# A third of the feed-forward units moved onto the score ring while attention runs

## Chip, core and metric

One core of a Trainium2 chip runs the whole program. The metric is device time in microseconds (us) of one execution; lower is better. TensorE is called PE below, VectorE DVE, ScalarE ACT, GpSimdE POOL, and the queue that issues the transfers SP, as in the profile.

## What is computed

```python
def reference(q, k, v, g_q, g_k, moe_w_in, moe_w_out, moe_s, moe_b, moe2_w_in, moe2_w_out):
    # q, k, v: 4 batches, 12 heads, 448 positions, 64 wide, float32
    q_n, k_n = rmsnorm(q, g_q), rmsnorm(k, g_k)
    attn = softmax(q_n @ k_n.T / sqrt(64))
    x = (attn @ v) gathered to 1792 tokens x 768
    h = x @ moe_w_in                       # 768 -> 2048
    x = (s * relu(h)**2 + b) @ moe_w_out   # 2048 -> 768
    h = x @ moe2_w_in
    return (h * cos(h)) @ moe2_w_out
```

Both feed-forward layers are computed with each operand split in a high and a low part, so each product is three matmuls (high by high, high by low, low by high).

## The kernel before

Attention goes by pairs of heads: 24 pairs, four score steps each, 96 steps in all. A step multiplies 112 rows of queries with all 448 keys for the two heads (tiles `sc`, line 193, two banks of PSUM), takes the row maximum on DVE (`top`, L205) and the exponential on ACT (`pr`, L208). Two steps later PE turns those rows over (`tp`, L226), and ACT copies the one head and DVE the other to SBUF (`pT`, L232 and L230). Once in a pair come the transposes of the next pair's queries and keys (`pt_q`, `pt_k`, L173), that of the reciprocals (`rt`, L237) and the product with the values (`av`, L249).

A feed-forward unit of the first layer is either an in-unit (`ph`, L400: 18 matmuls into one bank, from one block of 128 hidden columns and one batch) or an out-unit (`po`, L452: 6 matmuls into one bank, from a chunk of two such blocks). After an in-unit ACT takes the relu (`r`, L411), POOL squares it (L413), DVE scales it (`gt`, L415), ACT rounds it to its high part (`gh`, L429) and POOL makes the low part (`gl`, L430); `gh` and `gl` are what the out-units of that chunk read. After an out-unit ACT copies (first chunk, L458) or DVE adds (L461) the bank into `acc`. Weights are loaded ahead by `load_weight` into three buffers of each part (`wh`, `wl`): ACT writes the high part (L338), POOL the low part (L339), in two halves of 384 columns.

The first nine pairs run alone. From then on the generator of attention steps and the list of feed-forward units are woven by rates, until the attention is done; the last units of that stretch are those of segment 2. After that the score and transpose banks are given back and six banks with the tags `ph` and `po` (pool `psb`) take their place for the rest.

While attention runs PSUM's eight banks are: two with the tag `mo` (pool `psm`), four with the tag `sc` and two with the tag `tp`. In the woven part all feed-forward units share the two `mo` banks, the scores the four `sc` banks, and `pt`, `tp`, `rt` and `av` the two `tp` banks. The order on each engine is not that of the code: a scheduler sets it when the program is built, and each engine then runs its list in order, waiting on semaphores. A tile takes its bank when the scheduler places its first instruction, so a unit that has no bank is placed later than units behind it.

Of the kernel before, what the change touches and what calls it, by code (L numbers as in the profile page):

```python
# [33 lines left out]
def body(ctx, tc, q, k, v, g_q, g_k, w1_in, w1_out, s_in, b_in, w2_in, w2_out, out):  # L34
# [27 lines left out]
    psm = ctx.enter_context(tc.tile_pool(name="psm", bufs=2, space=PSUM))  # L62
# [28 lines left out]
    pools = {}  # L91
# [9 lines left out]
    def products(w, x):  # L101
        return ((w[0], x[0]), (w[1], x[0]), (w[0], x[1]))
# [229 lines left out]

    weights = {}
    plain = {}
    count = {"g": 0, "raw": 0}

    def halves(w, wh, wl, eng=nc.gpsimd):
        nc.scalar.copy(wh, w)  # L338
# [46 lines left out]
    g = {}  # L385
    acc = {}
    visits = {}
    pair = []

    def unit_in(layer, seg, ck, f, b):  # L390
        ft = ck * CF + f
        key = f"{layer}_{ft}_{b}"
        wh, wl = weights[layer, seg, 0, ft, 0]
        wh, wl = (z.rearrange("p (c f) -> p c f", f=P) for z in (wh, wl))
        pool, tag, bufs = (pools["psb"], "ph", 3) if "psb" in pools else (psm, "mo", 2)
        ph = pool.tile([P, 512], F32, tag=tag, name=f"ph_{key}", bufs=bufs)
        h = ph[:, :S]
        for c in range(NE):
            for n, (a, m) in enumerate(products((wh[:, c, :], wl[:, c, :]), xs[layer, b][c])):
                nc.tensor.matmul(h, a, m, start=(c == 0 and n == 0), stop=(c == NE - 1 and n == 2))  # L400
            if c % 2 and c < NE - 1:
                yield 1.13
        if count["g"] % 2 == 0:
            n = count["g"] // 2
            gp, nb = (ma, 3) if "mb" not in pools or n % 5 < 3 else (pools["mb"], 2)
            pair[:] = [gp.tile([P, 2, S], F32R, tag=f"g{z}", name=f"g{z}_{key}", bufs=nb) for z in "hl"]
        gh, gl = (z[:, count["g"] % 2, :] for z in pair)
        count["g"] += 1
        if layer == 0:
            r = ma.tile([P, S], F32, tag="t0", name=f"r_{key}")  # L410
            nc.scalar.activation(r, h, AF.Relu)  # L411
            r2 = ma.tile([P, S], F32, tag="t1", name=f"r2_{key}")
            nc.gpsimd.tensor_tensor(r2, r, r, ALU.mult)  # L413
            gt = ma.tile([P, S], F32, tag="t2", name=f"gt_{key}")
            nc.vector.tensor_scalar(gt, r2, sb[:, 0:1], sb[:, 1:2], ALU.mult, ALU.add)  # L415
        else:
            hs = ma.tile([P, S], F32, tag="t0", name=f"hs_{key}")
            nc.scalar.copy(hs, h)  # L418
            h = hs
            kk = ma.tile([P, S], F32, tag="t1", name=f"kk_{key}")  # L420
            nc.scalar.activation(kk, h, AF.Copy, scale=1.0 / (2 * math.pi), bias=MAGIC)
            nc.scalar.activation(kk, kk, AF.Copy, bias=-MAGIC)
            gt = ma.tile([P, S], F32, tag="t2", name=f"gt_{key}")
            nc.vector.scalar_tensor_tensor(gt, kk, -C1, h, ALU.mult, ALU.add)
            nc.vector.scalar_tensor_tensor(gt, kk, -C2, gt, ALU.mult, ALU.add)  # L425
            nc.scalar.activation(gt, gt, AF.Abs)
            nc.scalar.activation(gt, gt, AF.Sin, scale=-1.0, bias=halfpi)  # L427
            nc.gpsimd.tensor_tensor(gt, h, gt, ALU.mult)  # L428
        nc.scalar.copy(gh, gt)  # L429
        nc.gpsimd.tensor_tensor(gl, gt, gh.bitcast(F32), ALU.subtract)  # L430
        g[ft, b] = (gh, gl)
        if layer == 1 and b % 2:
            g[ft, "pair", b // 2] = [z.rearrange("p b s -> p (b s)") for z in pair]
        yield 1.13
# [3 lines left out]
        yield 1.13  # L438

    def po_tile(key):  # L440
        pool, tag, bufs = (pools["psb"], "po", 3) if "psb" in pools else (psm, "mo", 2)
        return pool.tile([P, 512], F32, tag=tag, name=f"po_{key}", bufs=bufs)

    def unit_out_1(seg, ck, et, b):
        key = f"0_{ck}_{et}_{b}"
        cols = et % (NE // 2)
        w = weights[0, seg, 1, ck, et // (NE // 2)]
        w = [z.rearrange("p (f c e) -> p f c e", f=CF, e=P)[:, :, cols, :] for z in w]
        po = po_tile(key)[:, :S]
        for f in range(CF):  # L450
            for n, (a, m) in enumerate(products([z[:, f, :] for z in w], g[ck * CF + f, b])):
                marks["out"] = nc.tensor.matmul(po, a, m, start=(f == 0 and n == 0), stop=(f == CF - 1 and n == 2))  # L452
        visits[et, b] = visits.get((et, b), 0) + 1
        if visits[et, b] == 1:
            if et % 2 == 0:
                acc[et // 2, b] = ma.tile([P, 2 * S], F32, tag="acc", name=f"acc_{key}", bufs=NE)
            at = acc[et // 2, b][:, et % 2 * S:(et % 2 + 1) * S]
            nc.scalar.copy(at, po)  # L458
            return
        at = acc[et // 2, b][:, et % 2 * S:(et % 2 + 1) * S]  # L460
        nc.vector.tensor_tensor(at, po, at, ALU.add)  # L461
        if visits[et, b] < NCK:
            return
        if b < 2:
            t = dram.tile([P, S], F32, tag=f"y_{b}_{et}", name=f"yd_{b}_{et}")
            nc.sync.dma_start(t, at)
            stash[1, b, et] = t
        else:
            xs.setdefault((1, b), []).append(split(at, xa, f"2_{b}_{et}", nc.vector if et % 4 < 2 else nc.gpsimd))

    def unit_out_2(seg, ck, eh, t):
        key = f"1_{ck}_{eh}_{t}"
        w = [z.rearrange("p (f e) -> p f e", f=CF) for z in weights[1, seg, 1, ck, eh]]
        pr, j0 = t // NT, t % NT * P
        po = po_tile(key)[:, :EH]
        for f in range(CF):
            x = [z[:, j0:j0 + P] for z in g[ck * CF + f, "pair", pr]]
            for n, (a, m) in enumerate(products(x, [z[:, f, :] for z in w])):
                nc.tensor.matmul(po, a, m, start=(f == 0 and n == 0), stop=(f == CF - 1 and n == 2))  # L479
        if ck == 0 and eh == 0:  # L480
            pool, nb = (ma, NE) if t < NE else (pools["mb"], 2 * NT - NE)
            acc[t] = pool.tile([P, E], F32, tag="acc", name=f"acc_{key}", bufs=nb)
        at = acc[t][:, eh * EH:(eh + 1) * EH]
        if ck == 0:
            nc.scalar.copy(at, po)
        else:
            nc.vector.tensor_tensor(at, po, at, ALU.add)  # L487
        if ck < NCK - 1 or eh == 0:
            return
        j = j0  # L490
        while j < j0 + P:
            b, c, p = 2 * pr + j // S, j % S // CP, j % CP
            n = min(CP - p, j0 + P - j)
            rows = out[b * S:(b + 1) * S, :].rearrange("(p c) e -> c p e", c=NCH)[c, p:p + n, :]
            nc.sync.dma_start(rows, acc[t][j - j0:j - j0 + n, :])
            j += n
# [153 lines left out]
```

## Time and profile before

| | us |
|---|---|
| median of three runs | 1315.49 |
| lowest and highest of them | 1313.4, 1315.62 |
| the profiled execution, device time | 1311.19 |
| its span, first to last instruction | 1309.4 |
| PE busy in that span | 1246.8 |

The profile tells of one execution. "Busy" of an engine is the time in which at least one of its instructions ran; the matmuls of a stream overlap, so the distance of their starts, not their length, is what one of them costs. The mean granted clock of PE over the span is 0.996 of full speed.

### The profile page before, as it was taken

How to read it: one execution, taken by the hardware profiler on the slowest of the kernel's cores; microseconds unless marked ns; L12 is line 12 of the kernel's file. 1: busy time of each engine (PE TensorE's matmuls, PEld its weight loads, DVE VectorE, ACT ScalarE, POOL GpSimd, SP SyncE). 2: the span in 40 equal slices, each digit the busy share in tenths (PEclk: the TensorE clock that was granted, in tenths of full speed). 3: DMA queues.
4: the chain of work that ended last, by engine and by line, in shares of the span. 5: the costliest groups of instructions: out<-in, count | busy, mean ns of one | idle time of the engine just before them, and what ended most of it. 6: DMA issues, size and time to landing. Idle time of an engine off the chain costs nothing.

```text
span 1309.4 us, 18684 instructions
## 1 busy us (share of the span) xinstructions
PE 1246.8 (95%) x6624; PEld 1033.3 (79%) x6624; DVE 845.8 (65%) x1452; ACT 755.4 (58%) x1694; POOL 569.6 (43%) x624
## 2 busy tenths in 40 slices
PE   5998899899999999999999999999999999999998
PEld 2444565676776767779999999989999999999997
DVE  5787674867768685754454445764767767666655
ACT  5787685666556655534432224788656657565641
POOL 3445454644536524234332223555544435354531
PEclk9999999999999999999999999999999999999999
DMA  3324252433433333253221222121212211111105
GB/s 102 94 87 125 83 151 59 137 123 115 125 113 104 120 104 114 68 185 117 89 70 49 66 63 64 47 61 49 66 32 73 66 56 49 49 50 49 49 13 169
DMA packets 81534, 111.33 MB, mean 85 GB/s; under 512 B 7200, under 2 KB 71456, under 8 KB 81440
## 3 DMA queue, kind: packets, MB, share of 16 engines
q1 hardware_dynamic: 81440, 110.13, 28.0%
q8 instruction: 52, 0.85, 0.3%
q14 instruction: 42, 0.34, 0.1%
HBM read 86.51 MB, written 23.59 MB: 84 GB/s over the span
## 4 chain that ended last, share of the span: by engine, by line
PE 67%; ACT 11%; DVE 10%; DMA 5%; POOL 3%; issue 3%; SPq 0%; ACTq 0%; DVEq 0%; POOLq 0%
PE ph L400 26%; PE po L479 14%; PE po L452 13%; PE av L249 5%; PE sc L193 4%; PE tp L226 3%; ACT pr L208 3%; DMA raw<-in_moe_w_out_dram 2%; DVE t L375 2%; DVE top L205 2%; DMA xr<-xd 1%; DMA raw<-in_moe_w_in_dram 1%; DVE gt L425 1%; ACT c L371 1%; ACT pT L232 1%
## 5 line engine op out<-in xcount | busy, mean ns | idle before, releaser
L400 PE MATMUL ph<-xh,wl 128*128 128x448 f32 x768 | 282.8, 368 | 0.0
L400 PE MATMUL ph<-xh,wh 128*128 128x448 f32 x768 | 280.1, 369 | 2.3 <-ACT hs L418 2.2
L400 PE MATMUL ph<-xl,wh 128*128 128x448 f32 x768 | 281.9, 368 | 0.0
L430 POOL TENSOR_TENSOR gl<-gt,gh 128x448 fp32r<-128x448 f32 x128 | 158.9, 1246 | 184.4 <-ACT gh L429 184.3
L339 POOL TENSOR_TENSOR wl<-t,wh 128x384 fp32r<-128x384 f32 x128 | 138.5, 1102 | 78.7 <-ACT wh L338 78.6
L208 ACT ACTIVATE pr<-sc,top 112x448 f32<-112x448 f32 x192 | 121.1, 636 | 66.8 <-DVE top L205 66.3
L400 PEld LDWEIGHTS ph<-xh,wh 128*128 128x128 f32 x768 | 144.2, 188 | 19.2 <-ACT hs L418 3.3
L479 PE MATMUL po<-wh,gh 128*128 128x384 f32 x448 | 152.1, 340 | 4.1 <-DVE acc L487 2.6
L452 PE MATMUL po<-gh,wh 128*128 128x448 f32 x384 | 145.5, 381 | 10.2 <-DVE acc L461 8.2
L400 PEld LDWEIGHTS ph<-xh,wl 128*128 128x128 f32 x768 | 144.3, 188 | 12.8 <-issue 2.7
L400 PEld LDWEIGHTS ph<-xl,wh 128*128 128x128 f32 x768 | 144.3, 188 | 12.3 <-issue 2.0
L461 DVE TENSOR_TENSOR acc<-po,acc 128x448 f32<-128x448 f32 x168 | 102.9, 618 | 77.5 <-PE po L452 77.4
L479 PE MATMUL po<-wh,gl 128*128 128x384 f32 x448 | 149.7, 334 | 0.0
L479 PE MATMUL po<-wl,gh 128*128 128x384 f32 x448 | 149.5, 334 | 0.0
L338 ACT CAST wh<-t 128x384 fp32r<-128x384 f32 x200 | 94.6, 512 | 85.9 <-PE po L452 47.9
L452 PE MATMUL po<-gl,wh 128*128 128x448 f32 x384 | 141.3, 368 | 0.0
L205 DVE TENSOR_REDUCE top<-sc 112x1 f32<-112x448 f32 x192 | 112.5, 615 | 44.3 <-PE sc L193 44.1
L452 PE MATMUL po<-gh,wl 128*128 128x448 f32 x384 | 141.0, 367 | 0.0
L487 DVE TENSOR_TENSOR acc<-po,acc 128x384 f32<-128x384 f32 x196 | 105.2, 550 | 48.9 <-PE po L479 48.6
L371 ACT ACTIVATE c<-raw 128x384 f32<-128x384 f32 x128 | 71.0, 555 | 109.6 <-DMA raw<-in_moe_w_out_dram 44.4
L226 PEld LDWEIGHTS tp<-ident,pr 112*112 112x112 f32 x768 | 79.0, 134 | 70.0 <-issue 21.4
L428 POOL TENSOR_TENSOR gt<-hs,gt 128x448 f32<-128x448 f32 x64 | 77.9, 1217 | 120.3 <-ACT gt L427 115.6
(82 smaller groups left out, 2243.4 us busy)
## 6 DMA issues: line engine op xcount, KB each, us to landing
raw<-in_moe_w_in_dram SPq DMA_DIRECT2D x64, 384.0 KB, 3.4
raw<-in_moe_w_out_dram SPq DMA_DIRECT2D x64, 384.0 KB, 3.2
t<-wd SPq DMA_DIRECT2D x72, 192.0 KB, 2.4
wd<-t SPq DMA_DIRECT2D x64, 192.0 KB, 3.5
rawq<-in_q_dram SPq DMA_DIRECT2D x24, 224.0 KB, 2.7
rawk<-in_k_dram SPq DMA_DIRECT2D x24, 224.0 KB, 2.9
rawv<-in_v_dram SPq DMA_DIRECT2D x24, 224.0 KB, 3.4
xd<-xf SPq DMA_DIRECT2D x12, 224.0 KB, 3.3
```

The costliest lines, as they stand in the source:

```text
L205: line("DVE", nc.vector.tensor_reduce(tops[j], sc[j], axis=AX.X, op=ALU.max, negate=True))
L208: e = line("ACT", nc.scalar.activation(pr, sc[j], AF.Exp, bias=tops[j], scale=1.0, accum_out=st[i]["sums"][:, c, j:j + 1]))
L226: mm = [nc.tensor.transpose(tp[:, kc * CP:(kc + 1) * CP], pr[:, kc * CP:(kc + 1) * CP], ident[:CP, :CP]) for kc in range(NCH)]
L338: nc.scalar.copy(wh, w)
L339: eng.tensor_tensor(wl, w, wh.bitcast(F32), ALU.subtract)
L371: for z in (nc.scalar.activation(cf, hi.bitcast(F32), AF.Copy, scale=2.0**-112), nc.scalar.activation(t, lo, AF.Copy, scale=LSCALE, bias=- ...
L400: nc.tensor.matmul(h, a, m, start=(c == 0 and n == 0), stop=(c == NE - 1 and n == 2))
L430: nc.gpsimd.tensor_tensor(gl, gt, gh.bitcast(F32), ALU.subtract)
L452: marks["out"] = nc.tensor.matmul(po, a, m, start=(f == 0 and n == 0), stop=(f == CF - 1 and n == 2))
L461: nc.vector.tensor_tensor(at, po, at, ALU.add)
L479: nc.tensor.matmul(po, a, m, start=(f == 0 and n == 0), stop=(f == CF - 1 and n == 2))
L487: nc.vector.tensor_tensor(at, po, at, ALU.add)
```

## The change

While `psb` is not open, a counter runs over all feed-forward units, in-units and out-units alike, in the order in which the code creates them. Every third takes a bank with the tag `sc` from the four that the scores use; the other two take `mo` as before. There are 128 such units; 42 of them go to the score ring and 86 stay.

```diff
-    count = {"g": 0, "raw": 0}
+    count = {"g": 0, "raw": 0, "sum": 0}
...
+    def sum_bank():
+        count["sum"] += 1
+        return (pools["ps"], "sc", 4) if count["sum"] % 3 == 0 else (psm, "mo", 2)
+
     def unit_in(layer, seg, ck, f, b):
...
-        pool, tag, bufs = (pools["psb"], "ph", 3) if "psb" in pools else (psm, "mo", 2)
+        pool, tag, bufs = (pools["psb"], "ph", 3) if "psb" in pools else sum_bank()
         ph = pool.tile([P, 512], F32, tag=tag, name=f"ph_{key}", bufs=bufs)
...
     def po_tile(key):
-        pool, tag, bufs = (pools["psb"], "po", 3) if "psb" in pools else (psm, "mo", 2)
+        pool, tag, bufs = (pools["psb"], "po", 3) if "psb" in pools else sum_bank()
         return pool.tile([P, 512], F32, tag=tag, name=f"po_{key}", bufs=bufs)
```

No instruction is added or taken away; the lists are put in another order between the first out-units and the last units of segment 2. On PE both lists read alike up to the first `po` and again from the first in-units of segment 3 on. The diff adds four lines above line 390, so L400, L452 and L193 of before are L404, L456 and L193 after it. Three places on PE show what moved. In the names `po_c_e_b` is chunk, output block and batch, `ph_f_b` hidden block and batch, `sc_p_s_j` pair of the batch, step and head; the last number counts tiles.

First place, the second score step of pair 5 of the second batch, shortly after the weaving begins. Before:

```order
L193 MATMUL sc_5_1_0_2075<-kT_5_1900,qT_5_1871 112x448
L193 MATMUL sc_5_1_1_2076<-kT_5_1900,qT_5_1871 112x448
L226 MATMUL tp_4_3_0_2087<-ident,pr_4_3_0_1964 112x112 x4
L452 MATMUL po_0_4_0_2417<-gh_0_0_1948,wh_0_1_0_1_1819 128x448
...
L452 MATMUL po_0_5_0_2529<-gl_0_0_1949,wh_0_1_0_1_1819 128x448
L226 MATMUL tp_4_3_1_2093<-ident,pr_4_3_1_1966 112x112 x4
L173 MATMUL pt_k_0_2105<-ident,nk_0_1647 128x112 x4
L193 MATMUL sc_5_2_0_2110<-kT_5_1900,qT_5_1871 112x448
L193 MATMUL sc_5_2_1_2111<-kT_5_1900,qT_5_1871 112x448
```

And with the change:

```order
L193 MATMUL sc_5_1_0_2075<-kT_5_1900,qT_5_1871 112x448
L193 MATMUL sc_5_1_1_2076<-kT_5_1900,qT_5_1871 112x448
L226 MATMUL tp_4_3_0_2087<-ident,pr_4_3_0_1964 112x112 x4
L226 MATMUL tp_4_3_1_2093<-ident,pr_4_3_1_1966 112x112 x4
L173 MATMUL pt_k_0_2105<-ident,nk_0_1647 128x112 x4
L193 MATMUL sc_5_2_0_2110<-kT_5_1900,qT_5_1871 112x448
L193 MATMUL sc_5_2_1_2111<-kT_5_1900,qT_5_1871 112x448
L456 MATMUL po_0_0_0_2198<-gh_0_0_1948,wh_0_1_0_0_1791 128x448
```

Twelve matmuls of two out-units stood between the two transposes and are gone from there; `po_0_0_0`, the first out-unit of all and the third unit of the count, now starts behind the scores of this step; before, it started four score steps earlier.

Second place, chunk 4, first batch of the pair: the last matmul of the in-unit `ph_9_1` and the out-units that read what is made of it. Before, the last row here stands 63 rows behind the first:

```order
L400 MATMUL ph_9_1_4782<-xl_1_5_2438,wh_1_0_9_0_4420 128x448
L400 MATMUL ph_10_0_4876<-xh_0_0_460,wh_1_0_10_0_4537 128x448
...
L400 MATMUL ph_10_1_4983<-xh_1_0_1402,wh_1_0_10_0_4537 128x448
...
L193 MATMUL sc_0_3_0_4149<-kT_0_3738,qT_0_3693 112x448
...
L452 MATMUL po_4_0_1_5018<-gh_8_0_4269,wh_1_1_4_0_4612 128x448
...
L452 MATMUL po_4_0_1_5018<-gh_9_0_4742,wh_1_1_4_0_4612 128x448
```

And with the change, where it stands 17 rows behind:

```order
L404 MATMUL ph_9_1_4782<-xl_1_5_2438,wh_1_0_9_0_4420 128x448
L226 MATMUL tp_2_2_0_4807<-ident,pr_2_2_0_4667 112x112 x4
L226 MATMUL tp_2_2_1_4813<-ident,pr_2_2_1_4669 112x112 x4
L456 MATMUL po_4_0_1_5018<-gh_8_0_4269,wh_1_1_4_0_4612 128x448
...
L173 MATMUL pt_q_4_4885<-ident,nq_4_4370 128x112 x4
L193 MATMUL sc_3_1_0_4890<-kT_3_4671,qT_3_4598 112x448
...
L226 MATMUL tp_2_3_0_4902<-ident,pr_2_3_0_4758 112x112 x4
L456 MATMUL po_4_1_0_5051<-gh_8_0_4269,wh_1_1_4_0_4612 128x448
...
L226 MATMUL tp_2_3_1_4908<-ident,pr_2_3_1_4760 112x112 x4
L456 MATMUL po_4_0_1_5018<-gh_9_0_4742,wh_1_1_4_0_4612 128x448
```

The two in-units of block 10 no longer stand between `ph_9_1` and its reader, because `ph_9_1` came late itself.

Third place, chunk 6, where the out-units pass from one half of the output weights (`wh_1_1_6_0`) to the other (`wh_1_1_6_1`). Before:

```order
L452 MATMUL po_6_2_1_6074<-gl_13_0_5878,wh_1_1_6_0_5798 128x448
L226 MATMUL tp_4_2_1_5377<-ident,pr_4_2_1_5219 112x112 x4
L193 MATMUL sc_5_1_0_5412<-kT_5_5221,qT_5_5148 112x448
L193 MATMUL sc_5_1_1_5413<-kT_5_5221,qT_5_5148 112x448
L226 MATMUL tp_4_3_0_5422<-ident,pr_4_3_0_5334 112x112 x4
L452 MATMUL po_6_3_0_6082<-gh_12_0_5541,wh_1_1_6_1_5914 128x448
```

And with the change:

```order
L456 MATMUL po_6_2_1_6074<-gl_13_0_5878,wh_1_1_6_0_5798 128x448
L456 MATMUL po_6_3_0_6082<-gh_12_0_5541,wh_1_1_6_1_5914 128x448
L456 MATMUL po_6_3_1_6100<-gh_12_0_5541,wh_1_1_6_1_5914 128x448
L456 MATMUL po_6_4_0_6118<-gh_12_0_5541,wh_1_1_6_1_5914 128x448
L456 MATMUL po_6_5_0_6162<-gh_12_0_5541,wh_1_1_6_1_5914 128x448
L404 MATMUL ph_15_1_6207<-xh_1_0_1402,wh_1_0_15_0_5762 128x448
```

In both programs `wh_1_1_6_1` lies in the buffer that `wh_1_1_6_0` leaves. The attention work that stood between the last reader of the one and the first reader of the other is no longer there.

## Rows read from the trace of the kernel before

**Rows 1.** The page: busy time of the engines, share of the span, instructions.

```profile
PE 1246.8 (95%) x6624; PEld 1033.3 (79%) x6624; DVE 845.8 (65%) x1452; ACT 755.4 (58%) x1694; POOL 569.6 (43%) x624
```

**Rows 2.** Stretches in us: all engines' busy time (instructions), granted clock, DMA share, GB/s.

```profile
0.00:156.30 156.30, 126.29 (x745) 64.37 (x745) 111.58 (x213) 112.21 (x307) 67.28 (x126) 0.98 0.35 102
156.30:541.00 384.70, 366.17 (x2007) 265.71 (x2005) 269.69 (x477) 236.47 (x580) 180.38 (x219) 1.00 0.36 110
541.00:640.00 99.00, 96.09 (x482) 85.27 (x481) 52.69 (x85) 45.78 (x96) 38.69 (x35) 1.00 0.42 131
...
600.00:620.00 20.00, 20.00 (x100) 18.55 (x99) 10.11 (x13) 11.59 (x24) 13.82 (x12) 1.00 0.41 121
...
640.00:1310.00 670.00, 658.29 (x3399) 617.93 (x3397) 411.86 (x680) 360.94 (x714) 283.21 (x245) 1.00 0.20 60
```

**Rows 3.** Waits of PE, 156 to 545 us: total, times, longest.

```profile
PE po L452 <- DVE acc L461: 5.4, 4, 2.2
PE rt L237 <- ACT pT L232: 3.5, 3, 1.9
PE rt L237 <- DVE pT L230: 2.0, 1, 2.0
PE tp L226 <- ACT pT L232: 1.9, 1, 1.9
PE po L452 <- ACT r L411: 1.3, 1, 1.3
```

**Rows 4.** Waits of PE, 545 to 640 us.

```profile
PE po L452 <- DVE acc L461: 2.8, 3, 1.5
```

**Rows 5.** PE in order of time: start, length; a stretch without idle.

```profile
159.19 0.36 PE L400 MATMUL ph<-xl,wh 128*128 128x448 f32 x1
159.40 0.36 PE L400 MATMUL ph<-xh,wh 128*128 128x448 f32 x1
...
160.61 0.55 PE L173 MATMUL pt_q<-ident,nq 112*128 112x112 f32 x4
161.09 1.01 PE L193 MATMUL sc<-kT,qT 64*112 64x448 f32 x4
162.03 0.60 PE L226 MATMUL tp<-ident,pr 112*112 112x112 f32 x4
162.39 0.45 PE L400 MATMUL ph<-xh,wh 128*128 128x448 f32 x1
```

**Rows 6.** PE in order of time, with [idle before]: all its idle in steps of few feed-forward matmuls.

```profile
171.62 0.60 PE L237 MATMUL rt<-ident,rb 112*128 112x112 f32 x4 [1.97 <-DVE pT L230]
...
213.91 0.60 PE L173 MATMUL pt_k<-ident,nk 112*128 112x112 f32 x4 [0.98 <-ACT pT L232]
...
217.00 0.57 PE L237 MATMUL rt<-ident,rb 112*128 112x112 f32 x4 [0.64 <-ACT pT L232]
...
226.47 0.60 PE L173 MATMUL pt_q<-ident,nq 112*128 112x112 f32 x4 [0.72 <-DVE pT L230]
...
527.93 0.67 PE L452 MATMUL po<-gh,wh 128*128 128x448 f32 x2 [0.24 <-ACT wh L338]
```

**Rows 7.** One pair of attention alone, in order of time: its scores, exponentials and idle.

```profile
61.21 1.01 PE L193 MATMUL sc<-kT,qT 64*112 64x448 f32 x4
...
65.10 1.01 PE L193 MATMUL sc<-kT,qT 64*112 64x448 f32 x4
...
66.80 0.64 ACT L208 ACTIVATE pr<-sc,top 112x448 f32<-112x448 f32 x1 [1.69 <-DVE top L205]
...
71.11 0.60 PE L226 MATMUL tp<-ident,pr 112*112 112x112 f32 x4 [0.54 <-DVE pT L230]
...
72.29 0.59 PE L226 MATMUL tp<-ident,pr 112*112 112x112 f32 x4 [0.59 <-ACT pT L232]
...
74.47 1.01 PE L193 MATMUL sc<-kT,qT 64*112 64x448 f32 x4
```

**Rows 8.** Groups by line, 156 to 541 us: busy, mean ns of one; idle before.

```profile
L339 POOL TENSOR_TENSOR wl<-t,wh 128x384 fp32r<-128x384 f32 x54 | 55.3, 1045 | 47.1 <-ACT wh L338 47.1
...
L338 ACT CAST wh<-t 128x384 fp32r<-128x384 f32 x54 | 25.1, 516 | 6.1 <-PE po L452 3.9 <-PE ph L400 2.1
```

**Rows 9.** From an in-unit's relu to its `gh` and `gl`, in order of time.

```profile
161.03 0.54 ACT L411 ACTIVATE r<-ph 128x448 f32<-128x448 f32 x1
164.94 0.57 ACT L429 CAST gh<-gt 128x448 fp32r<-128x448 f32 x1
...
236.14 0.52 ACT L411 ACTIVATE r<-ph 128x448 f32<-128x448 f32 x1
...
242.76 0.57 ACT L429 CAST gh<-gt 128x448 fp32r<-128x448 f32 x1
```

**Rows 10.** Stretches of 5 us around a stall of PE, columns as in rows 2.

```profile
360.00:365.00 5.00, 3.54 (x12) 3.14 (x12) 3.36 (x8) 3.33 (x10) 3.62 (x8) 0.74 0.27 97
365.00:370.00 5.00, 5.00 (x25) 1.71 (x24) 3.97 (x8) 1.70 (x3) 1.63 (x2) 0.92 0.58 160
```

**Rows 11.** Waits of ACT, 156 to 545 us.

```profile
ACT pr L208 <- DVE top L205: 38.0, 33, 4.3
```

## The prediction

> **What bounds the kernel now.** I read the page first: PE is busy 1246.8 us of the 1309.4 us span, every other engine 65% or less [rows 1]. So time can only be won or lost where PE stands idle. The table of stretches says where that is [rows 2]. While attention runs alone PE is busy 126.3 of 156.3 us. In the woven part, 156 to 541 us, it is busy 366.2 of 384.7 us: 18.5 us idle. From 541 to 640 us 2.9 us are idle. From 640 us on the change cannot act, since `psb` is open, and the two lists are alike there; before 156 us they are alike too. All that is at stake is the 21.4 us of idle between 156 and 640 us, and whatever new idle the order makes there.
>
> The waits of PE name the causes. In the woven part 5.4 us fall on out-units that wait for DVE to add an older unit from the same bank, 1.3 us on one that waits for a relu, and most of the rest on attention's own transposes, which wait until ACT or DVE has copied an older one out of the two `tp` banks [rows 3]. Behind the woven part the same add costs 2.8 us more [rows 4]. That is the picture that the change is about: feed-forward units wait for banks for 8.2 us, attention for about 11 us, and only the first of these is relieved by another bank.
>
> **The change, part by part.** No work is added, so PE's own work is the same and the sum is made of idle alone. The price of a matmul of a stream is the distance of two starts, 0.205 us; a step's scores cost 0.94 us, a group of transposes 0.36 to 0.48 us [rows 5].
>
> *What the order does.* Counting in the two lists, 960 feed-forward matmuls stand ahead of the last scores before, 792 after: the units that want a score bank get it late, what needs their weights and results comes later still, and 168 matmuls, 34 us, move behind attention. There PE works through them without attention; I cost that part at nothing because the trace has PE full from 600 to 620 us, where feed-forward work runs alone [rows 2]; its risk is named at the end.
>
> *Other lists.* SP's and POOL's lists change in the same window: loads of queries and keys stand earlier among the weight loads on SP, squares and low parts of late units stand behind attention's sums and norms on POOL. The transfers keep the DMA engines busy 0.36 of the woven part, POOL works 180 of its 385 us [rows 2]. I cost this at nothing by itself; where it would be late is in the weight and `gh` terms below.
>
> *Attention steps without filling.* A feed-forward matmul between two transposes hides the copy that the second waits for. The list has 55 score steps from the first in-unit on. Steps with six or fewer feed-forward matmuls behind their scores are 7 before and 15 after. The 7 cost 1.97, 0.98, 0.64, 0.72 and 0.24 us of idle, and nothing in two, 4.55 us in all [rows 6], 0.65 us each. Eight more make 8 x 0.65 = +5.2 us. Bounds: with ACT and DVE free of feed-forward work, a whole pair of four empty steps has 0.54 + 0.59 = 1.13 us of idle [rows 7], 0.28 us a step, so at least 8 x 0.28 = 2.3 us; at most the worst of the seven each time, 8 x 1.97 = 15.8 us. I take the mean since the new empty steps lie among feed-forward work, as those seven do. Queued behind such a transpose on PE are the next scores, so DVE's maximum and ACT's exponential move with it.
>
> *The add that PE waits for.* With a third of the units on other banks, two successive `mo` units may have a unit of the other ring between them, and the add of 0.6 us has 1.2 us more time. The lists show that this happens only in part: since the score-ring units come late and in clumps, `mo` units still follow each other. Places with less than 1.3 us of PE work between a unit's end and the next use of its bank or buffer are 11 before (10 of them in the clump of chunk 7, where the 2.8 us of [rows 4] lie) and 6 after; those of 1.3 to 2.5 us are 19 and 16. Bounds: 0, and all of 5.4 + 2.8 = 8.2 us [rows 3, 4]. I take -3 us, the clump.
>
> *Weights.* A late unit holds its weight buffer, one of three, so the refill starts late. By the buffers of the two programs, refills with under 8 us of PE work between the last reader of the old and the first reader of the new weights are 5 before and 14 after; the others have 9 to 37 us. A refill costs two casts of 0.516 us on ACT and two subtractions of 1.045 us on POOL [rows 8], about 3.1 us. Below that are 3 before and 4 after, the new one with no work at all between (the third place shown): its first matmul waits for one cast, 0.5 us and the hand-over; the low part is covered by the 4 + 18 matmuls ahead of it. Eight more lie between 3.1 and 8 us, covered unless ACT or POOL is late; I give them 0.2 us each. Sum +2 us. Bounds: 0, if all is covered, and one full refill plus a cast each, 3.1 + 8 x 0.516 = 7.2 us.
>
> *From in-unit to out-unit.* From the relu's start to the end of `gh` the trace has 4.5 us (161.03 to 165.51) in a quiet place and 7.2 us (236.14 to 243.33) in a busy one [rows 9]. In the list before, PE has 12 us or more of work between an in-unit's last matmul and the reader of its `gh` in every chunk but the first. After, four chunks have 4.9 to 7.0 us (the second place shown is the 4.85 us one). At most 7.2 - 4.85 = 2.35 us each, 9.4 us; at least nothing. I take a quarter, +2.4 us.
>
> *Scores on three banks.* Of the 188 times a score tile takes over a bank, all 188 in the list before take that of two steps ago; after, 140 do, 27 take the previous step's and 21 one that a feed-forward unit left. From the start of a step's scores to the end of its first exponential a quiet step needs 2.34 us (65.10 to 67.44) [rows 7]; the 27 have at least 3.8 us of PE work behind the tile whose bank they take. Nothing, then; the third rival prices the opposite.
>
> **Sum:** 5.2 - 3 + 2 + 2.4 = +6.6 us on the profiled execution's 1311.19 us, so 1317.8 us. The median of the runs shown is 4.3 us above that execution; the same offset gives **1322 us**. Low end of the terms: 2.3 - 8.2 = -5.9 us, 1309.6 us. High end: 15.8 + 7.2 + 9.4 = +32 us, which would need all at their worst.
>
> **Rivals.**
>
> *Relief wins.* The adds' 8.2 us go altogether, and empty steps cost only the 0.28 us of attention alone: -5.9 us, 1309.6 us. For it: those empty steps come with less feed-forward work on ACT and DVE, so copies may be prompt. Against it: the clumps in the list, and the idle in the empty steps of before. It decides if the new empty steps cost less than about 0.4 us each while the adds vanish. The Trainium skill, Perfetto Trace Analysis, Optimizing Tensor Performance, says that independent matmul groups should rotate through different PSUM banks so that evacuation overlaps the next group, and under Identifying Performance Opportunities that consistent bubbles can mean too little PSUM for the next tile. By that rule this rival is the forecast; the trace agrees with it for 8.2 us of waits and not for the 11 us of attention's. Chance 0.18.
>
> *No change.* PE's work is the same, and idle merely moves: the added 9.6 us of the other terms shrink to the 3 us that the adds give back. 1315.5 us, within 0.2% (2.6 us, about what a measurement of this kernel can tell from no change). Chance 0.17.
>
> *Scores wait for their banks.* ACT's exponential waits for DVE's maximum up to 4.3 us at a time [rows 11]. On the 7 reuses with 4.6 us or less of PE work, 2.34 + 4.3 - 4.6 = 2.0 us each is 14 us at worst; with all behind it late, the forecast would become about 1334 us. Against it: the shortest gap is 1.6 times the quiet latency. Chance 0.08.
>
> *The clock gives way.* At the 1.88 us stall of 361 us the granted clock read 0.74 and then 0.92 in two stretches of 5 us [rows 10], a loss of 5 x 0.26 + 5 x 0.08 = 1.7 us beside the stall. If each of eight new empty steps brought that, 13.6 us on top: 1336 us. Against it: over the whole woven part, the seven old empty steps included, the granted clock is 1.00 [rows 2]. The Trainium skill, TensorE: Matmul & The Clock Gate, describes such a failure, short idles between groups that cycle through PSUM banks, which make the clock fall back (A second HAM failure mode). The rows show one such dip here. Chance 0.07.
>
> **Numbers.** The forecast, +3 to +15 us, has 0.50. With the rivals: faster 0.18, same 0.17, slower 0.50 + 0.08 + 0.07 = 0.65. The range runs from the relief's 1309.5 to the clock's 1336 us; about 0.05 is left below and 0.1 above. The likeliest case's own range is 1318.5 to 1330.
>
> **What would show it.** In the changed kernel's profile PE idle between 156 and 640 us should be 25 to 33 us instead of 21.4; the last scores should end some 20 to 30 us earlier; the waits of `tp`, `pt`, `rt` and `av` should grow from 11 to 15 or more, and those of `po` for DVE shrink from 8.2 to about 5. New waits of `po` for ACT's or POOL's `gh`, `gl`, `wh` or `wl` should appear. Scores should show no wait of PE. I am wrong if attention's waits do not grow, or if the 34 us of feed-forward work behind attention shows idle of its own: there a weight load comes due sooner than anything before, and the trace before has no such stretch.

## The result, and the profile after

The change takes 1330.64 us (median of 4 runs, 1329.59 to 1333.92), the kernel before 1314.65 us beside it (4 runs): ratio 1.0121, 95% interval [1.0101, 1.0141]. That is 16.0 us more, where +6.6 us were forecast; the direction and the range (up to 1336 us) held, the size did not.

The page of the changed kernel has PE busy in this line:

```profile
PE 1259.0 (95%) x6624; PEld 1037.7 (78%) x6624; DVE 847.2 (64%) x1452; ACT 756.1 (57%) x1694; POOL 567.5 (43%) x624
```

Its busy time is 12.2 us above that of [rows 1] with the same 6624 matmuls: so part of the loss is no idle, but matmuls that take longer. The table of stretches, columns as in [rows 2]:

```profile
0.00:156.30 156.30, 127.14 (x736) 64.73 (x736) 109.79 (x211) 111.55 (x305) 67.08 (x125) 0.97 0.34 100
156.30:541.00 384.70, 357.99 (x1934) 252.58 (x1933) 264.13 (x462) 230.25 (x569) 167.47 (x209) 0.98 0.34 103
541.00:640.00 99.00, 94.60 (x456) 82.77 (x455) 56.09 (x91) 42.22 (x85) 44.24 (x41) 1.00 0.48 146
```

Idle is 26.7 us in the woven part and 4.4 us behind it, 31.1 in all instead of 21.4: +9.7 us. Beside that, the granted clock of the woven part is 0.98, where it was 1.00. The last score matmul starts at 524.1 us instead of 539.3, and the first matmul of the second layer's out-units at 877.6 instead of 856.5: attention is done sooner, the whole later.

The waits of PE from 156 to 545 us (total, times, longest):

```profile
PE rt L237 <- DVE pT L230: 3.6, 3, 2.0
PE po L456 <- ACT acc L462: 3.0, 2, 2.4
PE rt L237 <- ACT y L152: 2.4, 1, 2.4
PE pt_k L173 <- ACT pT L232: 2.3, 4, 1.0
PE tp L226 <- DVE xf L257: 2.1, 2, 1.1
PE po L456 <- DVE acc L465: 1.9, 2, 1.8
PE pt_q L173 <- ACT pT L232: 1.7, 1, 1.7
PE tp L226 <- DVE pT L230: 1.6, 1, 1.6
PE av L249 <- DVE pT L230: 1.6, 1, 1.6
...
PE po L456 <- POOL gl L434: 1.1, 2, 0.8
```

and from 545 to 660 us:

```profile
PE po L456 <- ACT gh L433: 1.7, 1, 1.7
PE po L456 <- ACT wh L338: 1.6, 1, 1.6
PE po L456 <- DVE acc L465: 1.0, 2, 0.8
```

Against [rows 3, 4]: the out-units' waits for DVE's add fall from 8.2 to 2.9 us, so the lent bank does what it can do. Attention's own waits (`rt`, `tp`, `pt_q`, `pt_k`, `av`) grow from 11.2 to 19.2 us (3.9 of it in shorter rows not shown), and out-units now wait for ACT's copy of a first chunk's sums (3.0 us; 0.3 before), for gates and for weights. Scores have no wait.

Counted by step (from the scores of one step to those of the next), the 15 steps with six or fewer feed-forward matmuls hold 17.7 us of attention's waits, 1.2 us each; the 7 of before held 4.3 us, 0.6 us each. In the fuller steps the same waits fell from 7.0 to 1.6 us.

Attention's long stalls lie in steps with little else on PE: 3, 6 and 2 feed-forward matmuls in the steps of these three. PE in order of time, with [idle before], beside [rows 6]:

```profile
226.55 0.86 PE L173 MATMUL pt_q<-ident,nq 112*128 112x112 f32 x4 [1.73 <-ACT pT L232]
...
434.80 0.84 PE L237 MATMUL rt<-ident,rb 112*128 112x112 f32 x4 [2.42 <-ACT y L152]
...
505.63 0.60 PE L226 MATMUL tp<-ident,pr 112*112 112x112 f32 x4 [1.64 <-DVE pT L230]
```

Each of these three matmul groups stands in a stretch of 10 us in which the granted clock fell; a fourth such place is at 267 us, where an out-unit waited 2.4 us for ACT's copy, a fifth in attention alone. Columns as in [rows 2]:

```profile
220.00:230.00 10.00, 7.27 (x35) 4.09 (x34) 6.48 (x14) 6.20 (x17) 1.96 (x3) 0.84 0.49 158
260.00:270.00 10.00, 7.43 (x34) 5.31 (x33) 9.97 (x18) 8.29 (x21) 6.25 (x6) 0.89 0.63 169
270.00:280.00 10.00, 10.00 (x48) 5.33 (x46) 5.81 (x11) 2.76 (x7) 4.61 (x9) 0.94 0.55 159
430.00:440.00 10.00, 7.58 (x36) 3.83 (x34) 9.23 (x16) 7.11 (x19) 7.91 (x11) 0.83 0.56 168
500.00:510.00 10.00, 8.36 (x40) 5.53 (x39) 9.47 (x18) 6.51 (x17) 4.85 (x5) 0.83 0.48 149
25.00:35.00 10.00, 7.99 (x43) 4.29 (x40) 6.97 (x14) 7.17 (x22) 6.92 (x16) 0.83 0.29 83
```

In the kernel before, each of these stretches has 1.00 granted, and only the dip of [rows 10] stands in the woven part. Length times (1 - clock) gives 1.6 + 1.1 + 0.6 + 1.7 + 1.7 = 6.7 us in the woven part, where it was 1.7, and 1.7 us more ahead of it: +6.7 us. At each of these places the clock stood for a part of the stretch at the lower of its two levels, 1.2 GHz; from 435.0 to 438.4 us, say, 0.50 is granted.

The length of a stall alone does not tell which of them brings a dip. In the kernel before, stalls of 1.97, 1.91, 2.21 and 1.88 us (171.6, 302.4, 415.4 and 465.7 us) each end amid ten microseconds with 1.00 granted, and one of 1.88 us has the dip of [rows 10]; in the change five stalls of 1.6 to 2.0 us between 156 and 640 us brought none.

A third part shows only in the order of time. The two halves of a step's scores (two heads, 64 rows of the array each) stood directly behind each other in all 96 steps before. In three steps of the change a feed-forward matmul got between them. A whole pair, then a split one:

```profile
222.18 1.01 PE L193 MATMUL sc<-kT,qT 64*112 64x448 f32 x4
223.12 0.47 PE L404 MATMUL ph<-xh,wh 128*128 128x448 f32 x1
223.43 0.37 PE L404 MATMUL ph<-xh,wl 128*128 128x448 f32 x1
...
278.57 1.00 PE L193 MATMUL sc<-kT,qT 64*112 64x448 f32 x2
279.51 0.47 PE L456 MATMUL po<-gh,wl 128*128 128x448 f32 x1
279.91 1.00 PE L193 MATMUL sc<-kT,qT 64*112 64x448 f32 x2
280.84 0.47 PE L456 MATMUL po<-gl,wh 128*128 128x448 f32 x1
```

A whole pair (x4) takes 0.94 us to the next start, one half alone (x2) takes 0.94 us too: the halves overlap fully when they are neighbours. The pair and one feed-forward matmul behind it take 223.43 - 222.18 = 1.25 us, the split one 280.84 - 278.57 = 2.27 us: 1.0 us each, 3.1 us for three. PE shows no idle there.

Over the whole span idle grows by 8.0 us, not 9.7, since PE idles 0.8 us less ahead of 156 us and 0.9 us less behind 640. Idle 8.0, clock 6.7, split pairs 3.1: 17.8 of the 20.1 us between the two profiled executions (1331.28 and 1311.19 us); 2.3 us of PE's busy time are not placed. The execution of before had a clock of 0.996 over its length, better than most (0.990 to 0.991 is the mean over the runs of before in the sets below, a loss of 11 to 13 us; the change loses 14.0); so in the medians, 16.0 us apart, the clock's share is nearer 1 to 3 us than 6.7.

### The profile page after: what moved, and what is told of

Read it like the earlier page. It is cut to its first block, busy times and chain, and to the rows that moved or that the text cites. A ratio compares the mean times of both kernels' runs of the same rounds, so it can differ in the third digit from the quotient of the medians.

```text
span 1329.5 us, 18674 instructions
## 1 busy us (share of the span) xinstructions
PE 1259.0 (95%) x6624; PEld 1037.7 (78%) x6624; DVE 847.2 (64%) x1452; ACT 756.1 (57%) x1694; POOL 567.5 (43%) x624
## 4 chain that ended last, share of the span: by engine, by line
PE 68%; ACT 11%; DVE 10%; DMA 5%; issue 4%; POOL 2%; SPq 0%; DVEq 0%; ACTq 0%; POOLq 0%
PE ph L404 26%; PE po L483 14%; PE po L456 13%; PE av L249 5%; PE sc L193 5%; PE tp L226 3%; ACT pr L208 3%; DVE t L375 2%; DMA raw<-in_moe_w_in_dram 2%; DVE top L205 1%; DVE gt L429 1%; ACT c L371 1%; DMA raw<-in_moe_w_out_dram 1%; DMA xr<-xd 1%; POOL wl L339 1%
## 5 line engine op out<-in xcount | busy, mean ns | idle before, releaser
L404 PE MATMUL ph<-xh,wl 128*128 128x448 f32 x768 | 283.3, 369 | 0.0
L404 PE MATMUL ph<-xl,wh 128*128 128x448 f32 x768 | 281.9, 367 | 0.0
L404 PE MATMUL ph<-xh,wh 128*128 128x448 f32 x768 | 279.8, 369 | 2.0 <-ACT hs L422 2.0
L339 POOL TENSOR_TENSOR wl<-t,wh 128x384 fp32r<-128x384 f32 x128 | 141.2, 1120 | 100.2 <-ACT wh L338 94.3
L404 PEld LDWEIGHTS ph<-xh,wh 128*128 128x128 f32 x768 | 144.3, 188 | 19.7 <-issue 4.6
L404 PEld LDWEIGHTS ph<-xh,wl 128*128 128x128 f32 x768 | 144.4, 188 | 13.6 <-issue 3.3
L456 PE MATMUL po<-gh,wh 128*128 128x448 f32 x384 | 144.5, 380 | 10.7 <-ACT acc L462 3.0
L404 PEld LDWEIGHTS ph<-xl,wh 128*128 128x128 f32 x768 | 144.4, 188 | 13.0 <-issue 2.7
L456 PE MATMUL po<-gl,wh 128*128 128x448 f32 x384 | 141.4, 371 | 1.1 <-POOL gl L434 1.1
L456 PE MATMUL po<-gh,wl 128*128 128x448 f32 x384 | 141.8, 370 | 0.0
```

The costliest lines, as they stand in the source:

```text
L339: eng.tensor_tensor(wl, w, wh.bitcast(F32), ALU.subtract)
```

## The experiments

Theory: late lent units leave steps of attention alone, and these cost idle. Rivals: scores miss the bank that they lend; each lent unit has a price of its own; the fixed order in which units follow one another is what hurts. The table has what was measured, beside what the profile of each shows: idle of PE from 156 to 640 us (the two stretches less PE's busy time), steps whose halves are split, and the loss to the clock (1 - clock, times the time, mean of the runs; before 11 to 13 us).

| version | ratio to before, interval | idle, us | split | clock, us |
|---|---|---|---|---|
| before | 1 | 21.4 | 0 | 11-13 |
| the change | 1.0121 [1.0101, 1.0141] | 31.1 | 3 | 14.0 |
| three score banks, none lent | 1.000 [0.9979, 1.0021] | 16.7 | 5 | 10.0 |
| lent units on a bank of their own | 0.9973 [0.9956, 0.999] | 12.3 | 14 | 7.6 |
| out-units alone | 1.0131 [1.0105, 1.0157] | 31.6 | 2 | 17.4 |
| in-units alone | 1.0088 [1.0061, 1.0115] | 29.9 | 2 | 10.6 |
| every sixth | 1.0211 [1.0183, 1.0238] | 39.5 | 3 | 18.5 |
| every second | 1.0041 [1.0027, 1.0055] | 26.1 | 2 | 8.5 |
| change, units in written order | 1.0212 [1.0189, 1.0235] | 37.6 | 0 | 25.5 |
| before, units in written order | 1.0004 [0.9992, 1.0017] | 20.5 | 0 | 14.3 |
| `tp` 3, `sc` 3, none lent | 1.0039 [1.0015, 1.0063] | 15.7 | 15 | 13.2 |
| the same, a third lent | 1.0121 [1.0104, 1.0139] | 13.5 | 31 | 12.7 |
| own bank, halves held back | 1.0028 [1.0009, 1.0046] | 23.4 | 0 | 14.2 |
| `tp` 3, a third lent, held back | 0.9962 [0.995, 0.9974] | 12.4 | 12 | 6.8 |
| `tp` 3, none lent, held back | 0.9942 [0.9924, 0.9959] | 19.6 | 0 | 8.9 |
| `tp` 2, `sc` 3, a third lent, held back | 1.0203 [1.0176, 1.023] | 27.7 | 7 | 22.2 |
| `tp` 2, `sc` 3, none lent, held back | 1.002 [1.0007, 1.0034] | 20.7 | 0 | 14.8 |
| the change, held back | 1.0128 [1.01, 1.0156] | 30.9 | 0 | 13.6 |

**Do the scores miss the bank?** The kernel before, with a ring of three and nothing lent:

```diff
-  sc = [ps.tile([P, 512], F32, tag="sc", name=f"sc_{key}_{j}", bufs=4)[:CP, :S] for j in range(2)]
+  sc = [ps.tile([P, 512], F32, tag="sc", name=f"sc_{key}_{j}", bufs=3)[:CP, :S] for j in range(2)]
```

> The kernel before, with three banks in the score ring instead of four and the fourth left empty; all feed-forward units stay on their two. Theory 'late units' (a unit that must win a bank from the scores is placed late, attention's steps go without filling, PE idles and its clock drops): nothing to win, so no late units; the list has 1004 feed-forward matmuls ahead of the last scores (960 before, 792 with the change) and 5 steps with six or fewer (7 before, 15 with the change), so 1310 to 1318 us. Theory 'scores lose a bank' (the slowness is attention on three banks): most of the 16 us, 1325 us or more, and waits of sc for pr in the trace.

1317.15 us against 1317.08, as the theory said: nothing. On balance the bank is free, so the rival that scores lack it falls. What moves cancels: idle is 4.7 us less and five pairs are split; ahead of 156 us PE is idle 21.2 us instead of 30.0, but the scores there keep it busy 53.2 us instead of 45.1, and the first in-unit starts at 157.6 us instead of 156.3.

**The same third of the units, on a bank that nothing else uses** (ring of three, and)

```diff
+  return (pools["ps"], "mx", 1) if count["sum"] % 3 == 0 else (psm, "mo", 2)
```

> As the change, every third unit on another bank, but that bank is its own (a ring of one) and the scores keep a ring of three. Late units: nobody competes for the bank, the list has 1098 feed-forward matmuls ahead of the last scores and 4 sparse steps, so 1304 to 1315 us, idle of PE from 156 to 640 us under 22 us, and at most one drop of the granted clock there. Scores lose a bank: 1325 us or more, as in the run with three score banks. Third theory, 'more feed-forward among the steps is itself the harm': also above 1320 us, with waits of attention's transposes grown.

1314.16 us against 1317.08. The two stretches that answer to [rows 2]:

```profile
156.30:541.00 384.70, 373.21 (x1974) 271.35 (x1973) 271.03 (x476) 234.64 (x574) 184.54 (x222) 1.00 0.37 112
541.00:640.00 99.00, 98.20 (x495) 78.69 (x494) 50.72 (x83) 44.51 (x99) 32.52 (x32) 1.00 0.38 118
```

12.3 us idle where the change has 31.1 and the ring of three alone 16.7. Units on a third bank are no harm; the harm goes with the ring that they share with the scores. That it comes from their lateness is not shown by this run alone, but fits the count: 1098 feed-forward matmuls stand ahead of the last scores here, 960 before, 792 in the change.

**Which units, and how many.** Every third out-unit alone, which lends 32 of the 96 out-units, then every third in-unit alone, 10 of the 32 in-units (the other call has `(psm, "mo", 2)` again):

> Every third out-unit on the score ring, in-units all on their two banks. Late units: 836 matmuls ahead of the last scores, 11 sparse steps, half way between the two kernels: 1319 to 1326 us. If what hurts is only that in-units (18 matmuls) hold a score bank for long: 1313 to 1317 us.

1335.75 us. Expected was half the loss; it is as slow as the change or slower, with a single wait of 4.5 us of an out-unit for DVE's add and a clock loss of 17.4 us.

> Every third in-unit on the score ring, out-units all on their two banks. Late units: 798 matmuls ahead of the last scores, 11 sparse steps: 1319 to 1328 us. If in-units that hold a bank are the whole cause: as the change, 1328 to 1333 us; if out-units are: 1313 to 1317 us.

1328.88 us, 1 us above the theory's range and in that of "in-units that hold a bank are the whole cause"; but with no in-unit lent the time was 1335.75 us, so that falls. So neither part of the lending gives a share of the loss that fits its number of units, though both lend about as many matmuls (192 and 180). Then every second and every sixth (`% 2`, `% 6`):

> Every second unit on the score ring, 64 of the 128. Late units by the count of sparse steps (780 matmuls ahead of the last scores, 12 sparse steps): 1322 to 1330 us, no worse than the change. Rival 'each lent unit costs' (16 us for 42): 1336 to 1342 us.

1320.87 us with 64 lent, 1 us under the theory's range and far below the rival's.

> The change with every sixth unit lent in place of every third (21 of 128 in place of 42). Steps with few sums: 11 (15 in the change, 7 before). Theory 'the loss follows the steps that run empty', which lie half-way: 1320 to 1326 us. Rival 'each lent unit costs alike' gives the same 1323, so this run tells only against a third: a few lent units are free, 1313 to 1318 us.

1344.01 us with 21 of 128 lent, a clear miss, in the other direction: fewer lent units, slower. None of the three candidates holds. A price for each lent unit is excluded, and the count of steps with few matmuls (11 here, 15 in the change, 12 with every second) does not order the times either. Idle and clock do: 39.5 and 18.5 us here, 26.1 and 8.5 there. That leaves which units are late, and where; the runs don't give a rule for it.

**Late units that the others queue behind.** The change, with all feed-forward units kept in the order in which they are written:

```diff
+  def in_line(mm):
+      if "psb" not in pools:
+          if behind:
+              issue_after(mm[0], behind[-1])
+          behind.append(mm[-1])
...
+  in_line(mms)
```

> The change, and in the woven part each feed-forward unit is ordered on PE behind the one before it, so a late unit is not overtaken but holds up all behind it. The list: 768 matmuls ahead of the last scores, 20 sparse steps, 14 of them empty. Theory late units leave steps unfilled: slower than the change, 1331 to 1345 us. Rival 'overtaking is the harm' (units out of order hold weights and results): faster than the change, 1314 to 1325 us.

1343.66 us. The first wait of PE in the woven part is now

```profile
PE pt_k L173 <- ACT pT L232: 10.9, 9, 3.1
```

where the change had 2.3. The control, the same edit on the kernel before:

> The kernel before (nothing lent, a score ring of four), with the feed-forward units' matmuls held to the order in which the units are written, as in the version of the change that took 1.0212. If that version lost by late lent units that the others had to queue behind: 1313 to 1320 us here. Rival 'the fixed order costs by itself, whatever the banks': 1323 to 1332 us.

1316.6 us against 1316.67. The fixed order costs nothing by itself; with lent units in it, it costs 12 us beyond the change. So the freedom to let other units pass a late one was hiding part of the price of lending.

**A third bank for the transposes.** If the price is paid in steps where a transpose waits for a copy out of one of two `tp` banks, a third should take it away. The score ring gives its free bank (`bufs=3` at `sc`), and

```diff
-  return ps.tile([P, 512], F32, tag="tp", name=name)
+  return ps.tile([P, 512], F32, tag="tp", name=name, bufs=3)
```

first with nothing lent, then with the change's lending:

> The kernel before, nothing lent, but the scores' ring has three banks and the ring of the transposes (tp, and pt, rt, av from pair 9 on) three instead of two. The list is sparse, as with the change: 756 feed-forward matmuls ahead of the last scores, 13 steps with six or fewer, 8 of them empty. Theory 'paid at the tp banks' (an empty step costs because a transpose waits for a copy out of one of only two banks): 1303 to 1316 us, the waits of PE's tp, pt, rt and av under 6 us in the woven part in place of 11 before and 19 with the change. Rival 'an empty step costs whatever the banks' (it waits for maximum and exponential): 1320 to 1328 us, as sparse as the change.

1320.29 us, outside the theory's range and at the low end of the rival's.

> The change's lending, every third unit on the score ring, with three score banks and three transpose banks. Late units as with the change: 758 matmuls ahead of the last scores, 12 sparse steps. Paid at the tp banks: the 8 us by which attention's waits grew go, so 1312 to 1322 us. Rival 'late units pay by themselves' (weights refilled late, gh and gl not ready, chunk copies, clock): most of the 16 us stay, 1324 to 1333 us.

1332.72 us, as the rival said. Yet the waits for `pT` are gone in both but for 0.3 us, and idle is half that of the change. Half of that idle is now the scores' own: they wait 7.6 and 7.8 us for ACT's exponential, which the change never shows. The order of time shows where the rest of the time is: 15 and 31 steps have their halves split. The reading is that with three banks the second half's bank often comes free later than the first's, and the scheduler puts other work in between. To try it, the first half is held back until the exponential that frees the second half's bank is done:

```diff
+  if s:
+      follow(mm[0], firsts[s - 1])
...
+  if j == 0:
+      firsts.append(e)
```

> Nothing lent, a score ring of three, three banks for the transposes, with the same holding back (15 split pairs with 162 matmuls between them before, now none). Theory 'split pairs were what that version lost': its 1320.3 less 7.5 us, 1309 to 1315 us. Rival 'waits of the scores for the exponentials cost the same however the pairs stand': 1318 to 1323 us, with over 6 us of waits of the scores for pr.

1308.0 us against 1316.67, 1 us under the expected range: the fastest version of all, 12.3 us below the one without the holding back.

> The change's lending out of a score ring of three, with the same holding back of the first half (31 split pairs with 262 matmuls between them before, now 12 with 55). Theory 'split pairs made that version slow': 19 x 0.5 = 10 us less than its 1332.7, so 1319 to 1325 us. Rival 'units that come late to a shared ring pay by themselves': 1329 to 1336 us.

1310.59 us, 22 us less than the version with 31 split pairs and 8 us under the expected range. The time saved, with the idle added and without the idle and the clock won back, over the split pairs that went, gives the price of a split in both couples: (12.3 + 3.9 - 4.3) / 15 = 0.8 us, and (22.1 - 1.1 - 5.9) / 19 = 0.8 us, above the 0.5 us that the expectation said. (Ahead of 156 us the idle differs too, but the first in-unit starts within 0.3 us of the same time in both of each couple.) The scores' own busy time from 156 to 640 us falls by 14.0 us in the first couple (70.3 to 56.3) and by 19.7 in the second (87.5 to 67.8): 0.9 to 1.0 us a pair, near the 1.0 us read above.

> The units on a bank of their own with a score ring of three (0.9973 of before), and the first half of each step's scores held back until the exponential that frees the second half's bank is done, so that the two halves stand directly behind each other in PE's order (in 14 of 96 steps other PE work stood between them, now in none). Theory 'a split pair costs about 0.5 us, since its halves no longer overlap': 14 x 0.5 = 7 us less, 1306 to 1311 us. Rival 'the work between the halves had to be done anyway, and a pair held back leaves PE without work': 1313 to 1320 us, with waits of the scores for pr of over 3 us.

1320.15 us: the theory's range fails, and the time is the upper end of the rival's, with 3.0 us of waits of the scores for `pr`. With two `tp` banks, the pair that is held back leaves PE without work (23.4 us idle instead of 12.3), which takes what the whole pairs give. In these runs whole pairs pay only where the transposes have three banks.

**Lending, with two and with three banks for the transposes.** The version at 0.9962, with two `tp` banks again (the diff above, reversed):

> The version that took 0.9962 (a third lent, a score ring of three, first halves held back) with two banks for the transposes again in place of three, and nothing else changed. Steps with at most 6 sum matmuls ahead of them: 17 (12 with the third bank). Theory 'the change loses in steps with few sums, by waits for the two transposes banks': 1325 to 1334 us, with over 12 us of PE's waits for pT and the copies behind the transposes. Rival 'holding the halves back is what cured it': 1308 to 1317 us.

1344.54 us; the rival (1308 to 1317) falls, and it is slower than the theory's range too. PE's waits from 156 to 660 us, of this version and then of the one with three `tp` banks:

```profile
PE sc L194 <- ACT pr L211: 4.4, 3, 3.0
...
PE pt_k L174 <- ACT pT L237: 2.3, 4, 1.0
PE av L254 <- DVE pT L235: 2.2, 3, 1.6
PE rt L242 <- ACT y L153: 2.2, 1, 2.2
PE po L461 <- ACT wh L343: 2.2, 2, 1.8
PE rt L242 <- DVE pT L235: 2.0, 1, 2.0
PE tp L231 <- DVE pT L235: 1.9, 1, 1.9
```

```profile
PE sc L194 <- ACT pr L211: 6.7, 5, 2.7
PE po L461 <- ACT wh L343: 2.0, 2, 1.5
PE po L461 <- DVE acc L470: 1.9, 3, 1.2
PE tp L231 <- ACT pT L237: 0.7, 1, 0.7
```

Attention's waits, those of the scores left aside, sum to 13.8 us in the first (with rows not shown) and to 1.5 us in the second. Without lending:

> Nothing lent, a score ring of three, two transposes banks, first halves held back: the version without lending beside the one with a third lent out of three. 8 steps with few sums (5 without the holding back, which took 1.000). Theory 'lending costs where the transposes have two banks': 1313 to 1320 us here, 10 us or more below the lent one. Rival 'lending costs only by the halves' place': both within 4 us of one another.

1319.8 us, in the theory's range; the same waits of attention sum to 9.0 us here, and to 2.6 us in the version without lending that has three `tp` banks. So the lending costs 1344.5 - 1319.8 = 24.7 us with two `tp` banks, and 1310.6 - 1308.0 = 2.6 us with three. Of the 24.7 us, 7.0 are idle, 7 x 0.8 = 5.6 split pairs and 7.4 the clock; 4.7 are not placed. The scheduler makes another order in each of the four, so this is what the banks do with all that follows from them, not one wait by itself.

Two things show when all runs are laid side by side. With two `tp` banks, the eight versions that lend out of the score ring take 1.0041 to 1.0212 of before, and the five that do not 0.9973 to 1.0028: that lending costs is not the luck of one order, though its size changes with the order. And the two versions that are held back and have three `tp` banks run faster than before with only 762 and 768 feed-forward matmuls ahead of their last scores, fewer than the change's 792: steps with little feed-forward work cost little where the transposes have a third bank and the pairs are whole.

**The change itself, held back:**

> The change itself (ring of four, two transposes banks), with each step's first half of the scores held back until the exponential of the step before is done for its first half; no split pairs (3 in the change). Steps with few sums: 16 (15 in the change). Theory 'waits for the two transposes banks in steps with few sums': as slow as the change, 1326 to 1334 us. Rival 'the halves' place did it': 1310 to 1318 us.

1333.41 us, as slow as the change. Its three split pairs are whole, and attention alone, ahead of the woven part, has 33.7 us idle instead of 29.2: what the one may give, the other takes back. So split pairs are not the main cause of the change's loss; whether they cost it the 3 us read above, this run can't tell.

## Why the prediction was off

**What held.** The idle of the woven part and behind it came to 31.1 us (25 to 33 said). Attention's waits grew from 11.2 to 19.2 (15 or more said), waits for gates and weights appeared, scores did not wait. The last scores came 15 us earlier, not 20 to 30.

**The terms of the sum, forecast and measured.** Steps without filling: +5.2, from 0.65 us a step; measured 1.2 us of attention's waits in each of 15, +13.4 us (4.3 to 17.7), inside the bounds. The fuller steps gave back 5.4 us (7.0 to 1.6), for which the sum had no term; +8.0 us together. The adds: -3, measured -5.3. Weights: +2, measured +1.4 (`wh`, 1.6 instead of 0.2). From in-unit to out-unit: +2.4, measured +2.8 (`gh` 1.7 and `gl` 1.1). Not in the sum at all: the copies of a first chunk's sums, +2.7. They add to +9.6 against 6.6. Misses of both signs partly cancel: that the idle came into its window is in part luck. This part of the sum was 3 us short between 156 and 640 us, and 1.4 us (8.0 against 6.6) over the whole span.

**The step that failed** is what the sum was made of: "the sum is made of idle alone", since "no work is added, so PE's own work is the same". PE's busy time grew by 12.2 us, more than its idle. Two things are seen to make the same work longer.

The first is the clock, which stood in a rival at 0.07 and in the sum at zero. Its price of 1.7 us a dip was right (1.6 to 1.7 us at each of the five places). Its argument against was that the woven part of before, old empty steps included, has 1.00 granted; but the new order brought more dips: four lie at stalls of 1.6 to 2.4 us, two of them longer than any of before's and two shorter. Four more dips came in the profiled pair, one of them ahead of the woven part, some 1 to 3 us in the medians; 25.5 us are lost where the units are kept in order. Which stalls bring a dip stays open. The Trainium skill, TensorE: Matmul & The Clock Gate (A second HAM failure mode), has short idles between groups that cycle through PSUM banks as a cause of such falls; the four dips of the woven part at stalls of 1.6 to 2.4 us agree with it, and the stalls of 1.6 to 2.2 us without a dip show that one such idle is not enough.

The second is the term of the scores on three banks, put at nothing. The forecast looked for a wait of the scores and rightly saw none; but the second half's bank can come free later than the first's, and the scheduler then puts other work in between, which costs 1.0 us without any idle. In the change this is three steps, 3.1 us.

As an estimate, since idle and pairs are read from one execution each and the clock from medians: of the 9.4 us by which the forecast fell short, 1.4 are idle, 3.1 split pairs and 1 to 3 the clock; the rest is not placed.

**The 168 matmuls behind attention, at nothing:** that stretch had 2.9 us of idle before and has 4.4 now: the `gh` and `wh` waits of the terms above, 3.3 us, are new there, and the adds give back 1.8. That is the idle of its own that was named as the risk, and it is small.

**The rivals.** Relief alone is real where the units have a bank of their own (0.9973); in the shared ring it gives back 5.3 us. The Trainium skill, Perfetto Trace Analysis (Optimizing Tensor Performance), would have groups rotate through different banks: the run with the own bank agrees, and the change, in which the bank is shared with scores, does not. That scores wait for their banks did not happen: the change has no such row, and a ring of three with nothing lent costs nothing. (The price given to this rival was added wrongly: 1322 + 14 is 1336 us, not 1334.)

**What stays open:** why every sixth unit lent costs more than every third, and every third more than every second. Among these versions idle and clock follow the times, but no count of the order that was tried foretells them.

## What to carry to other kernels

A bank that is free by its waits is not free to share: in this kernel the units that queue for it behind the scores come late, and attention's steps are left without cover. Give such units a bank of their own, or widen the ring that will then stall first (here the transposes: with whole pairs and three score banks the lending costs 24.7 us with two banks there, 2.6 with three). Do not sum idle alone: ask which new stalls may take the clock down (1.7 us a dip here), and whether matmuls that overlap stay neighbours in the order.

## What the runs showed of the hardware

Two matmuls of 64 rows each on the two halves of the array overlap fully when nothing stands between them: 0.94 us for both, 0.94 us for one. One other matmul between them costs the overlap: 1.0 us by the rows, 0.8 us by the runs' times, in busy time and not in idle. The Trainium skill, TensorE: Matmul & The Clock Gate (Why this matters for your kernels), says that small-K matmuls in distinct row groups run at the same time; the whole pair agrees, and that another matmul between them takes it away is shown by these runs.
